# Loading the first eight rows of k as fp32 on SyncE's queue, with casts on VectorE and ScalarE, and building the identity later

## The chip, the cores and the metric

The kernel runs on one core of one Trainium2 chip. The metric is the device time of one execution in microseconds (us), lower is better. Times are compared between executions of the same rounds on the same chip.

## The reference, cut to what matters

```python
# q, k, v: (4, 6144, 256) fp32; w1, w2, w3: (256, 768); w_out: (768, 256)
qn = q / (np.linalg.norm(q, axis=1, keepdims=True) + 1e-06)
kn = k / (np.linalg.norm(k, axis=1, keepdims=True) + 1e-06)
s = kn.transpose(0, 2, 1) @ qn / tau          # 256 x 256 for each of 4 batches
a = softmax(s)                                # over the last axis
x = (v @ a).reshape(24576, 256)
out = np.maximum(np.maximum(x @ w1, x @ w2), x @ w3) @ w_out
```

## The kernel before

Only the first batch concerns us: its k and q have to be loaded, all of them, before the first attention matrix exists. k and q lie in SBUF as fp8, and the cast is done by the DMA itself; these loads are issued by GpSimd (POOL). Each partition holds 48 rows of 256 columns.

```python
k_r = k.rearrange("b (p g) c -> b p g c", p=P)          # 48 rows g per partition

def load_k(b, g0, w):
    POOL.dma_start(out=qk[b][1][:, g0:g0 + w, :], in_=k_r[b][:, g0:g0 + w, :])

for load, widths in ((load_k, [4, 4] + [8] * 5), (load_q, [8] * 5 + [4, 2, 2])):
    g0 = 0
    for w in widths:
        load(0, g0, w)
        g0 += w
        if load is load_k and g0 == 8:
            ident = consts.tile([P, P], BF16, name="ident")
            make_identity(nc, ident)                     # two instructions on GpSimd
# ... then the weights and the first v tiles, on POOL too
```

TensorE multiplies k with itself (`kk`, for the norms) as the pieces land, then q with k (`gram`), makes the weights of the first half (`aw_half`), and works through v in chunks of 512 rows. The first v tile is transposed on TensorE, all others by a transposing DMA on SyncE's queue:

```python
aw_half(et, rinv, aw, 0, [2], lambda: v_transpose_pe(0))
v_transpose(1)                                           # SP.dma_start_transpose
# ... for each chunk gi:
    load_v(gi + 4)
    v_transpose(gi + 2)
    for fc in range(FC):
        h_block(gi, aw, fc)                              # 6 matmuls of 512 columns each
        for f in gaps[fc]:
            f()
```

## Time and profile before

| | before |
|---|---|
| time, 3 runs | 586.51 us (585.48 to 586.59) |
| span of the profiled run | 584.5 us |
| TensorE busy | 95% of the span |
| first traffic on the DMA engines | 2.60 us |
| last 8-row load of k taken up by TensorE | 20.10 us |
| transpose of the second v tile landed | 56.05 us |
| from there to the end | TensorE without a gap |

A trace is read here from its end: what must be earlier for the end to be earlier? The chain of waits answers that, and the windows (busy times and DMA rate of a stretch) tell what the stage in question is short of. The prediction shows the lines. In all lines from the profile, PE is TensorE, PEld its loading of weights, DVE VectorE, ACT ScalarE, POOL GpSimd and SP SyncE; a q behind the name (SPq) means the engine's instruction queue.

### The profile page before, as it was taken

How to read it: one execution, taken by the hardware profiler on the slowest of the kernel's cores; microseconds unless marked ns; L12 is line 12 of the kernel's file. 1: busy time of each engine (PE TensorE's matmuls, PEld its weight loads, DVE VectorE, ACT ScalarE, POOL GpSimd, SP SyncE). 2: the span in 40 equal slices, each digit the busy share in tenths (PEclk: the TensorE clock that was granted, in tenths of full speed). 3: DMA queues.
4: the chain of work that ended last, by engine and by line, in shares of the span. 5: the costliest groups of instructions: out<-in, count | busy, mean ns of one | idle time of the engine just before them, and what ended most of it. 6: DMA issues, size and time to landing. Idle time of an engine off the chain costs nothing.

```text
span 584.5 us, 9286 instructions
## 1 busy us (share of the span) xinstructions
PE 557.8 (95%) x3316; PEld 327.9 (56%) x3316; DVE 405.5 (69%) x623; ACT 305.6 (52%) x526; POOL 225.3 (39%) x232
## 2 busy tenths in 40 slices
PE   2786999999999999999999999999999999999997
PEld 2652555555575555555575555555575555555554
DVE  0035678778748787777848778777857777778775
ACT  0033357676735447767646446767745444444442
POOL 4241017877671006777770105777671000000000
PEclk9998899999999999999999999999999999999999
DMA  8999927988468635888649624899646344323211
GB/s 77 107 171 163 140 56 135 141 122 155 89 118 120 105 101 94 156 131 134 124 87 145 108 83 99 125 155 133 119 91 127 73 90 117 82 58 106 55 72 73
DMA packets 75134, 64.83 MB, mean 111 GB/s; under 512 B 52304, under 2 KB 61392, under 8 KB 75088
## 3 DMA queue, kind: packets, MB, share of 16 engines
q0 software_dynamic: 18400, 26.75, 38.8%
q1 hardware_dynamic: 56544, 37.23, 24.9%
q8 instruction: 26, 0.43, 0.3%
q10 hardware_dynamic: 144, 0.26, 0.1%
q14 instruction: 20, 0.16, 0.1%
HBM read 78.64 MB, written 25.17 MB: 178 GB/s over the span
## 4 chain that ended last, share of the span: by engine, by line
PE 90%; DMA 9%; POOL 1%; issue 0%; DVE 0%; POOLq 0%
PE h_ps L320 63%; PE o_ps L339 21%; DMA q_sb<-in_q_dram 3%; PE gram L226 3%; DMA vt_sb<-v_sb 2%; PE ew_ps L273 2%; DMA k_sb<-in_k_dram 2%; DMA v_sb<-in_v_dram 1%; PE o_ps L359 0%; POOL w_sb L128 0%; POOL k_sb L99 0%; PE n_ps L207 0%; PE n_ps L209 0%; DVE o_sb L365 0%; POOL ident masks.py:199 0%
## 5 line engine op out<-in xcount | busy, mean ns | idle before, releaser
L320 PE MATMUL h_ps<-vt_sb,aw_sb 128*128 128x512 bf16 x1728 | 409.0, 381 | 5.0 <-DMA vt_sb<-v_sb 5.0
L324 DVE TENSOR_TENSOR s_mx<-h_ps,s_mx 128x512 bf16<-128x512 f32 x288 | 197.8, 687 | 105.8 <-ACT s_mx L323 98.7
L320 PEld LDWEIGHTS <-aw_sb 128*128 128x128 bf16 x1728 | 168.8, 98 | 169.9 <-DMA vt_sb<-v_sb 5.5
L323 ACT ACTIVATE s_mx<-h_ps 128x512 bf16<-128x512 f32 x288 | 171.4, 595 | 138.8 <-PE h_ps L320 137.5
L325 DVE TENSOR_TENSOR ht_sb<-h_ps,s_mx 128x512 bf16<-128x512 f32 x288 | 199.3, 692 | 30.7 <-DVE s_mx L324 0.5
L195 POOL TENSOR_TENSOR acc<-acc,sq 128x768 f32<-128x768 f32 x90 | 147.5, 1650 | 70.8 <-ACT sq L189 70.6
L339 PE MATMUL o_ps<-wo_sb,ht_sb 128*128 128x256 bf16 x1128 | 154.0, 273 | 0.0
L339 PEld LDWEIGHTS <-ht_sb 128*128 128x128 bf16 x1128 | 110.5, 98 | 53.3 <-issue 0.6
L342 ACT ACTIVATE o_sb<-o_ps 128x512 f32<-128x512 f32 x94 | 56.1, 597 | 83.0 <-PE o_ps L339 83.0
L110 POOL DMA_DIRECT2D v_sb<-in_v_dram x48 | 26.7, 559 | 105.3 <-DMA vt_sb<-v_sb 101.6
L189 ACT ACTIVATE sq<-q_sb 128x768 bf16<-128x768 fp8e4 x48 | 40.5, 844 | 0.0
L189 ACT ACTIVATE sq<-k_sb 128x768 bf16<-128x768 fp8e4 x48 | 40.1, 835 | 0.0
L192 POOL CAST acc<-sq 128x768 f32<-128x768 bf16 x6 | 4.9, 820 | 74.7 <-ACT sq L189 74.7
L102 POOL DMA_DIRECT2D q_sb<-in_q_dram x32 | 17.6, 553 | 12.4 <-DMA k_sb<-in_k_dram 11.0
L157 PE MATMUL kk<-k_sb 128*128 128x256 fp8e4 x48 | 7.8, 339 | 13.6 <-DMA k_sb<-in_k_dram 13.6
L99 POOL DMA_DIRECT2D k_sb<-in_k_dram x31 | 17.0, 551 | 1.0 <-POOLq L439 0.8
L273 PE MATMUL ew_ps<-w_sb,et 128*128 128x384 bf16 x96 | 17.1, 326 | 0.0
L276 ACT ACTIVATE aw_sb<-ew_ps,rinv 128x384 bf16<-128x384 f32 x24 | 13.8, 581 | 6.1 <-PE ew_ps L273 5.1
L226 PE MATMUL gram<-k_sb,q_sb 128*128 128x512 fp8e4 x144 | 16.8, 276 | 0.0
L226 PEld LDWEIGHTS <-q_sb 128*128 128x256 fp8e4 x144 | 15.9, 136 | 0.6
L178 ACT ACTIVATE lnk<-kb_ps 128x256 f32<-128x256 f32 x1 | 0.4, 384 | 27.6 <-PE kb_ps L175 27.6
L157 PEld LDWEIGHTS <-k_sb 128*128 128x256 fp8e4 x48 | 6.5, 182 | 14.7 <-DMA k_sb<-in_k_dram 14.7
(49 smaller groups left out, 107.7 us busy)
## 6 DMA issues: line engine op xcount, KB each, us to landing
out_dram<-o_sb SPq DMA_DIRECT2D x47, 512.0 KB, 2.9
v_sb<-in_v_dram POOLq DMA_DIRECT2D x48, 256.0 KB, 4.0
k_sb<-in_k_dram POOLq DMA_DIRECT2D x24, 192.0 KB, 5.5
q_sb<-in_q_dram POOLq DMA_DIRECT2D x24, 192.0 KB, 7.0
k_sb<-in_k_dram POOLq DMA_DIRECT2D x5, 256.0 KB, 11.1
q_sb<-in_q_dram POOLq DMA_DIRECT2D x5, 256.0 KB, 19.4
w_sb<-in_moe_w_dram POOLq DMA_DIRECT2D x6, 192.0 KB, 8.9
vt_sb<-v_sb SPq DMA_TRANSPOSE x47, 3.7
```

What stands on the lines that cost most here:

```text
L102: POOL.dma_start(out=qk[b][0][:, g0:g0 + w, :], in_=q_r[b][:, g0:g0 + w, :])
L110: POOL.dma_start(out=t, in_=v_r[gi // NCH, gi % NCH])
L189: ACT.activation(out=sq, in_=src, func=AF.Square)
L195: POOL.tensor_tensor(out=acc, in0=acc, in1=sq, op=ALU.add)
L226: PE.matmul(g[:, j * C:(j + 1) * C], lhsT=qt[:, tsl, j * P:(j + 1) * P], rhs=kt[:, tsl, :], start=(tp == 0 and j == 0), stop=(tp == NG // ...
L273: PE.matmul(ew[:, :FH], lhsT=et[:, j, ic * P:(ic + 1) * P], rhs=w_sb[m][:, j, fsl], start=(j == 0), stop=(j == CC - 1))
L320: PE.matmul(t.rearrange("p (t n) -> p t n", t=TPC), lhsT=aw[m][:, ic, fsl], rhs=vt[:, :, ic, :], start=(ic == 0), stop=(ic == CC - 1))
L323: ACT.activation(out=s_mx, in_=hp[0], func=AF.Copy)
L324: DVE.tensor_tensor(out=s_mx, in0=hp[1], in1=s_mx, op=ALU.max)
L325: DVE.tensor_tensor(out=ht[:, fc, :], in0=hp[2], in1=s_mx, op=ALU.max)
L339: PE.matmul(st["ps"][:, half], lhsT=ht[:, fc, t * P:(t + 1) * P], rhs=wo_sb[:, fc, :], start=(fc == 0), stop=(fc == FC - 1))
L342: ACT.activation(out=st["o"][:, t - 1:t + 1, :].rearrange("p t d -> p (t d)"), in_=st["ps"], func=AF.Copy)
```

## The change

The intent: SyncE has nothing to do in the first 40 us. Its queue is to bring the first eight rows of k of each partition (a sixth of k), as they are in memory (fp32), while POOL's queue starts up. VectorE and ScalarE, idle at that time, cast half of them each. The identity matrix, which GpSimd builds, leaves the start of POOL's stream.

```diff
     alloc_qk(0)
-    for load, widths in ((load_k, [4, 4] + [8] * 5), (load_q, [8] * 5 + [4, 2, 2])):
-        g0 = 0
+
+    HEAD = 8
+    kf = consts.tile([P, HEAD, C], FP32, name="kf")
+    HH = HEAD // 2
+    for i in range(2):
+        SP.dma_start(out=kf[:, i * HH:(i + 1) * HH, :], in_=k_r[0][:, i * HH:(i + 1) * HH, :])
+    for load, widths in ((load_k, [8] * 5), (load_q, [8] * 5 + [4, 2, 2])):
+        g0 = HEAD if load is load_k else 0
         for w in widths:
             load(0, g0, w)
             g0 += w
-            if load is load_k and g0 == 8:
+            if load is load_q and g0 == 8:
                 ident = consts.tile([P, P], BF16, name="ident")
                 make_identity(nc, ident)
@@ ... @@
     DVE.memset(warm, 0.0)
+
+    DVE.tensor_copy(out=qk[0][1][:, 0:HH, :], in_=kf[:, 0:HH, :], saturate=False)
+    ACT.activation(out=qk[0][1][:, HH:HEAD, :], in_=kf[:, HH:HEAD, :], func=AF.Copy, saturate=False)
```

## The prediction

> **What bounds the kernel now.** I read the page first, then the chain of waits up to 70 us, the half-microsecond windows, and the timeline of the first stage. The page puts 90% of the chain that ended last on TensorE and 9% on DMA; POOL has 1%:
>
> ```profile
> PE   2786999999999999999999999999999999999997
> ...
> PE 90%; DMA 9%; POOL 1%; issue 0%; DVE 0%; POOLq 0%
> ```
>
> From the fourth slice on (a slice is 14.6 us) TensorE is 90% busy or more, so a change in the first microseconds can only move the moment at which that steady part begins. The chain, in order of time, says what sets that moment:
>
> ```profile
> 3.01 0.49 POOL k_sb L99
> 3.50 9.21 DMA k_sb<-in_k_dram
> ...
> 12.99 20.07 DMA q_sb<-in_q_dram
> ...
> 35.54 8.08 DMA v_sb<-in_v_dram
> ...
> 43.63 12.41 DMA vt_sb<-v_sb
> ...
> 56.09 5.30 PE h_ps L320 x12
> ```
>
> To be seen (the pieces before 3.01 are the first POOL issues at 1.23 and 1.89 and the building of the identity): apart from issues, everything up to 56 us is transfers. They are k, q, the weights, v, then the transpose of the second v tile, which shares the DMA engines with loads already in the queue. TensorE waits 5.0 us for that transpose and then runs to the end. So the quantity that matters is when the DMA stream gets through a fixed amount of data.
>
> Windows (columns: stretch, its length, busy time and count of PE, PEld, DVE, ACT and POOL, PE clock, DMA share, GB/s):
>
> ```profile
> 2.00:2.50 0.50, 0.00 (x0) 0.00 (x0) 0.00 (x0) 0.01 (x1) 0.50 (x2) 1.00 0.00 0
> 2.50:3.00 0.50, 0.00 (x0) 0.00 (x0) 0.00 (x0) 0.00 (x0) 0.42 (x3) 1.00 0.78 20
> ...
> 6.00:6.50 0.50, 0.01 (x1) 0.01 (x1) 0.00 (x0) 0.00 (x0) 0.50 (x2) 1.00 1.07 61
> ...
> 2.50:10.00 7.50, 1.50 (x8) 1.13 (x8) 0.00 (x0) 0.00 (x0) 4.64 (x10) 1.00 1.01 84
> 10.00:20.00 10.00, 5.02 (x32) 4.28 (x32) 0.00 (x0) 0.00 (x0) 2.12 (x4) 1.00 1.06 107
> ```
>
> No byte moves before 2.5 us, although the first load is issued at 1.23. The GB/s count the fp8 bytes written, a quarter of the fp32 bytes read, so 107 means 428 GB/s read. That rate then holds from 10 to 30 us without a gap: the stream is limited by what is read, and the queue never runs dry. The mean from 2.5 to 10 us is only 84.
>
> **What the Trainium skill says.** "DMA: Bandwidth & Descriptors", section "Issuing engines are not separate DMA queues": DMAs issued from different engines run on the same 16 DMA engines and interleave; only the sequencer's issue time is saved. So a second queue buys no rate where the windows show 428 GB/s read, only the time in which the first queue has not begun. The trace of the kernel before agrees as far as it goes: the v transposes on SyncE are slow, 12.41 us, exactly while POOL loads are in flight.
>
> The same page, "Specifications", gives a first byte after about 1 us for the GpSimd path and 0.6 us for the SyncE path. This trace has both longer: POOL's load, issued at 1.23, shows traffic from the window at 2.5 us on; an output store, issued by SyncE at 79.05, shows its first traffic in the window 79.75 to 80.00 (229 GB/s), and 410 in the next quarter. So about 0.8 against 1.3 us; I use these.
>
> "SBUF — State Buffer", section "SBUF: two separate sides", warns that an fp32 copy on VectorE between SBUF tiles locks GpSimd out of a shared port and stalls its descriptor writing. The change adds one such copy. The kernel before has none at this place, so its trace says nothing here.
>
> "TensorE: Matmul & The Clock Gate", section "Part 1: The HAM clock gate": an idle window of about 3.4 us halves the clock, and a sustained busy one of that length restores it. This trace agrees:
>
> ```profile
> 51.20:54.60 3.40, 0.00 (x0) 0.00 (x0) 1.48 (x3) 0.00 (x0) 0.00 (x0) 1.00 1.13 115
> 54.60:58.00 3.40, 1.91 (x5) 0.74 (x6) 0.00 (x0) 0.60 (x1) 1.43 (x3) 0.51 1.17 171
> 58.00:61.50 3.50, 3.50 (x10) 1.31 (x9) 2.13 (x4) 0.60 (x1) 1.75 (x4) 0.50 1.05 120
> 61.50:65.00 3.50, 3.50 (x23) 2.10 (x22) 2.02 (x3) 1.46 (x3) 0.00 (x0) 1.00 1.10 139
> ```
>
> TensorE is idle from 51.1 to 56.1, the clock is 0.5 from about 54.65 to 61.5, and the work from 56.1 to 61.5 runs at half speed: 5.4 us, of which 2.7 are lost.
>
> **The change, part by part.**
> *Removed*: two POOL loads of k, four rows per partition each. In the chain they are issued at 1.23 and 1.89, about 0.53 us apiece, 1.2 us of POOL's stream together.
> *Moved*: the identity (0.22 and 0.29 us with gaps, 0.54 together) goes behind the first q load. VectorE needs it first at 21.5 us, so it stays hidden. POOL now issues k rows 8 to 15 at 1.23 instead of 3.0. Beyond that the order of POOL's issues is the same, and each load still waits for the landing of the one eight before it, as before.
> *Added on SyncE*: two fp32 loads of 512 KB. The other engines get past the start barrier at 0.73 to 0.83 us; SyncE should issue at about 0.8, so its first bytes come at about 0.8 + 0.8 = 1.6. The bytes read from HBM are the same as before; the writes are four times larger for this sixth of k, at 410 GB/s by the store's window, near the 428 of the stream.
> *Added casts*: VectorE's tensor ops grow from 284 ns at 128 columns to 687 at 512, about 1.05 ns a column, so 1,024 columns cost at most 1.2 us, less if the copy runs in a faster mode. ScalarE grows from 595 ns at 512 to 840 at 768, so about 1.1 us. VectorE is otherwise idle until 21.5 us and ScalarE until 29.6. The casts let TensorE begin on k, but TensorE then waits for every later 8-row load (1.2 us of every 2.46) and for the q landing, so the casts are off the path unless they last several microseconds.
>
> Gain of the stream, against full rate (107 GB/s in written bytes):
> 1. Earlier start: 2.5 to about 1.65, less 0.1 for the SyncE queue's own ramp: 0.75 us.
> 2. Ramp of the POOL queue, 2.5 to 5.5 us: six windows of 20, 49, 86, 102, 105, 104 are 233 KB against 321, so 88 KB or 0.82 us. The SyncE queue has about 0.65 of its 1 MB left then and can fill it; I take 0.7.
> 3. The dip from 5.5 to 9.5 us (86, 61, 70, 90, 94, 90, 98, 111; 350 KB against 428): 0.73 us. I see no cause for it, so I count a third, 0.25.
> Sum: 1.7 us, with a floor near 0.9 and a ceiling near 2.3. Every later transfer and TensorE's restart at 56.1 should move by that.
>
> **The clock step.** The restart meets the clock gate's windows. If their edges stay at 51.24, 54.65, 58.07 and 61.48 us (multiples of 3.41 from the span's start fit all the clock changes), then with a shift over 1.4 us TensorE restarts before 54.65, at 54.4. The window up to 54.65 is still nearly all idle, so the clock drops; the next is fully busy, so it is restored at 58.07 instead of 61.48. That loses 1.7 instead of 2.7 us and adds 1.0 to the gain: 2.7 in all. With a shift under 1.4 us the clock is restored at 61.48 as before, and half of the shift is lost at half clock: 0.5 to 0.7 gained.
>
> **Rivals.**
> (a) *Rigid shift, same clock loss*: 1.7 us gained, 584.8. For it: the loss is tied to the idle length if the windows float from run to run, as the skill page says. Against it: the runs before lie within 1.1 us, which floating windows would hardly allow.
> (b) *No throttle*: the few tenths of work before the window's edge are enough to keep the clock, or the idle gap falls across two windows. The whole 2.7 comes back: 4.4 in all, 582.1. Against it: such a window is 90% idle.
> (c) *Hidden anyway*: the two queues only interleave and the ramp is HBM's, not the queue's; shift below 1.4, gain about 0.6, 585.9. For it: the dip at 6 us comes with the queue already full.
> (d) *A new wait*: the VectorE copy holds POOL's descriptor writing, or the casts hold TensorE. At most 1.2 us at about 4 us, while several loads are queued and TensorE has slack: 0 to +0.5, up to 587. I see no engine that becomes the bound.
>
> **Range and chances.** Weights: the main line at 583.8 about 0.4, (a) 0.15, (b) 0.2, (c) 0.2, (d) 0.05. The weighted mean is 584.2. The middle eight tenths run from (b) to just past (c): 581.9 to 586.1. Two per cent is 11.7 us, several times the largest gain I can add up and more than everything before the first byte, so the chance of "same" is nearly one: 0.985, faster 0.01, slower 0.005.
>
> **What would show it.** Right: traffic from about 1.6 us; the last 8-row k load, which TensorE takes up at 20.10 now, at 18.4 (17.8 to 19.2); the 2.46 us spacing unchanged; the v transpose landing near 54.4 instead of 56.05, still about 12 us long; the clock restored near 58 us; the rest of TensorE's work equally long. The step on the ramp is wrong if traffic starts early but the last k load shifts by under 1 us; the step on the clock is wrong if the half-clock stretch is as long as before or absent. The whole is wrong if the transpose at the end of the load phase does not move with the k loads, for then something other than the stream sets it, or if the SyncE loads run well under 400 GB/s.

## The result

The changed kernel took 585.21 us (median of 4 runs, 584.16 to 585.65), the kernel before in the same rounds 586.0 us (584.98 to 586.59). The ratio is 0.9986, with a 95% interval of 0.9965 to 1.0007. A ratio is the mean time of one kernel's runs over that of the other's runs in the same rounds, so it is not quite the ratio of the medians. Executions over 1.5% slower than the fastest of the same kernel are left out of the means. Two later timings, of five executions each, gave 0.9979 (0.9967 to 0.9992) and 0.998 (0.9966 to 0.9993). The gain is therefore real but small: 0.8 to 1.3 us by the three pairs of means, and "the same" at 2%.

The chain of waits of the changed kernel, in order of time (columns: start, length, what):

```profile
1.23 1.19 POOL k_sb L99 x2
2.42 10.76 DMA k_sb<-in_k_dram
...
13.47 18.73 DMA q_sb<-in_q_dram
...
33.87 8.08 DMA v_sb<-in_v_dram
...
41.97 12.85 DMA vt_sb<-v_sb
...
54.87 4.87 PE h_ps L329 x12
```

The v load is issued 1.67 us earlier than before (33.87 against 35.54), it takes 8.08 us as before, and TensorE restarts 1.22 us earlier (54.87 against 56.09). The transpose in between took 12.85 us instead of 12.41.

The half-microsecond windows of the changed kernel (columns as in the prediction; the last is GB/s as written):

```profile
1.50:2.00 0.50, 0.00 (x0) 0.00 (x0) 0.00 (x0) 0.50 (x1) 0.50 (x2) 1.00 0.81 98
2.00:2.50 0.50, 0.00 (x0) 0.00 (x0) 0.00 (x0) 0.02 (x1) 0.50 (x2) 1.00 0.77 156
2.50:3.00 0.50, 0.00 (x0) 0.00 (x0) 0.00 (x0) 0.00 (x0) 0.50 (x2) 1.00 0.78 221
...
3.50:4.00 0.50, 0.00 (x0) 0.00 (x0) 0.00 (x0) 0.00 (x0) 0.50 (x2) 1.00 0.99 401
...
6.00:6.50 0.50, 0.12 (x1) 0.00 (x0) 0.00 (x0) 0.50 (x1) 0.50 (x1) 1.00 0.97 98
```

Until about 5 us this is fp32, so the figure is also what is read; at 6 us it is fp8, and 98 means 392 GB/s read. Traffic starts in the window at 1.5 us. The new queue needs the same two microseconds to come up to its rate as POOL's did. And the dip is gone: 98 where the kernel before had 61.

The timeline of the changed kernel's start (columns: start, length, engine, line, instruction, count, and in brackets the idle time before it and what ended it):

```profile
0.74 0.87 SPq L119 DMA_DIRECT2D kf<-in_k_dram  x2
...
4.62 0.69 DVE L152 CAST k_sb<-kf 128x1024 fp8e4<-128x1024 f32 x1 [3.34 <-DMA kf<-in_k_dram]
4.84 0.63 POOL masks.py:199 TENSOR_SCALAR_AFFINE_SELECT ident<-ident 128x128 bf16<-128x128 bf16 x1
...
5.37 0.75 PE L166 MATMUL kk<-k_sb 128*128 128x256 fp8e4 x4 [5.37 <-DVE k_sb L152]
...
5.82 1.06 ACT L153 ACTIVATE k_sb<-kf 128x1024 fp8e4<-128x1024 f32 x1 [3.80 <-DMA kf<-in_k_dram]
...
18.10 1.25 PE L166 MATMUL kk<-k_sb 128*128 128x256 fp8e4 x8 [1.21 <-DMA k_sb<-in_k_dram]
```

The first matmul starts at 5.37 us, slightly later than before (5.24), because the cast stands before it; the last piece of k is taken up at 18.10 instead of 20.10. The same line of the kernel before:

```profile
20.10 1.26 PE L157 MATMUL kk<-k_sb 128*128 128x256 fp8e4 x8 [1.20 <-DMA k_sb<-in_k_dram]
```

Following the matmuls one by one through the two traces shows where the shift was lost and won. TensorE is ahead by 2.0 us at the end of k, by 1.96 at the end of q, by 1.66 in the first v chunk, by 1.22 at the restart, by 1.76 from 62 us on, and then by 1.76 at every matmul I compared up to the last one at 578.27 us. The span is shorter by only 1.4 us (584.5 to 583.1). So 0.54 us came back at 60 us and 0.37 us were lost behind the last matmul. The first is the clock:

```profile
51.20:54.60 3.40, 0.00 (x0) 0.00 (x0) 0.00 (x0) 0.00 (x0) 0.00 (x0) 0.67 1.21 112
54.60:58.00 3.40, 3.13 (x8) 1.16 (x9) 1.04 (x2) 0.60 (x1) 2.65 (x6) 0.50 0.86 168
58.00:61.50 3.50, 3.50 (x18) 1.70 (x16) 1.74 (x4) 1.19 (x2) 0.53 (x1) 0.83 1.09 110
```

In these windows of the changed kernel the clock (third number from the end) averages 0.67 in the first stretch. If it was 1 for a time and 0.5 for the rest, it was 1 for (0.67 - 0.5) / 0.5 x 3.4 = 1.16 us and fell near 52.36; the clock records say 52.35. It came back at 59.17 us. TensorE worked 4.30 us of that time at half speed and lost 2.15 us, where it had lost 2.7 before.

The second is the end of the program. SyncE's waits for the output stores at the end, before and after (columns: total, times, longest):

```profile
SPq L453 <- DMA out_dram<-o_sb: 1.7, 2, 1.1
```

```profile
SPq L462 <- DMA out_dram<-o_sb: 2.1, 2, 1.4
```

SyncE ends the program by checking the eight counters of its and ScalarE's DMAs, one after the other. The DMAs take the counters in turn, so the two added loads move every later store two places on. In the kernel before the last two stores sit on the last two of the eight counters, and nothing is left to check when they have landed. In the changed kernel they sit on the first two. SyncE comes to them 0.4 us earlier, so its waits are longer, and the wait for the last store ends at the same distance from the last matmul (3.56 us after its start in both). But six more checks of 0.06 us each follow. From the start of the last matmul to the last instruction it is 4.39 to 4.42 us in all seven traces of kernels without the SyncE loads, and 4.77 to 4.80 us in all six with them (fast executions). No run changed this order alone.

### The profile page after: what moved, and what is told of

Its sections match the earlier page's. It is cut to its first block, busy times and chain, and to the rows that moved or that the text cites. A ratio compares the mean times of both kernels' runs of the same rounds, so it can differ in the third digit from the quotient of the medians.

```text
span 583.1 us, 9290 instructions
## 1 busy us (share of the span) xinstructions
PE 557.3 (96%) x3316; PEld 327.7 (56%) x3316; DVE 406.2 (70%) x624; ACT 306.7 (53%) x527; POOL 224.6 (39%) x230
## 4 chain that ended last, share of the span: by engine, by line
PE 90%; DMA 9%; POOL 0%; issue 0%; DVE 0%; POOLq 0%
PE h_ps L329 63%; PE o_ps L348 21%; DMA q_sb<-in_q_dram 3%; PE gram L235 3%; DMA vt_sb<-v_sb 2%; PE ew_ps L282 2%; DMA k_sb<-in_k_dram 2%; DMA v_sb<-in_v_dram 1%; PE o_ps L368 0%; POOL w_sb L134 0%; PE n_ps L216 0%; POOL k_sb L99 0%; PE n_ps L218 0%; DVE o_sb L374 0%; PE rs_ps L270 0%
## 5 line engine op out<-in xcount | busy, mean ns | idle before, releaser
L235 PE MATMUL gram<-k_sb,q_sb 128*128 128x512 fp8e4 x144 | 16.8, 276 | 0.0
L178 PE MATMUL gram<-k_sb,q_sb 128*128 128x512 fp8e4 x48 | 10.8, 322 | 3.3 <-DMA q_sb<-in_q_dram 3.3
L288 DVE TENSOR_SCALAR aw_sb<-ew_ps,rinv 128x384 bf16<-128x384 f32 x24 | 13.4, 609 | 0.5 <-PE ew_ps L282 0.5
```

The lines of the kernel that those rows point to most:

```text
L235: PE.matmul(g[:, j * C:(j + 1) * C], lhsT=qt[:, tsl, j * P:(j + 1) * P], rhs=kt[:, tsl, :], start=(tp == 0 and j == 0), stop=(tp == NG // ...
```

## The experiments

Every trace gives two measures that vary less than the times: when TensorE takes up the last 8-row load of k, and when POOL's queue has written a given amount. In the three traces of the changed kernel they lie within 0.06 and 0.08 us, but in the two traces with the identity alone moved within 0.96 and 0.26. For the second measure I count POOL's packets by their start, with 256 KB added where SyncE brought the first eight rows (6,000 KB are of 1,024 bytes here). Times of single executions carry about half a microsecond of chance. All twelve runs gave correct results. Six of them were executed once, for the trace; their times are not used.

### The kernel before, once more (before_again)

No edit.

> The kernel before, unchanged, for the repeatability of what I read from one profile. Expected: TensorE takes up the last 8-row k load at 20.10 us within 0.1, the dip in the written rate between 5.5 and 9.5 us is there again (about 88 GB/s mean against 107), the v transpose lands within 0.3 us of 56.05. If the clock gate's windows float from run to run, the half-clock stretch starts somewhere else than at 54.65 us, or with another length of work in it; if they are fixed to the start of the program, it is 54.65 again.

The last k load is taken up at 20.14 us, the rate from 5.5 to 9.5 us is 86 GB/s (88 in the first trace), and 6,000 KB are reached at 48.81 us (48.62). These repeat. The restart doesn't, quite: 56.75 us against 56.09. The half-clock stretch lies at 53.64 to 60.46 us instead of 54.65 to 61.48, and costs 1.9 us instead of 2.7. The clock's windows float.

### The identity alone moved (ident_only, ident_only_timed)

```diff
-            if load is load_k and g0 == 8:
+            if load is load_q and g0 == 8:
```

> The kernel before with one part of the change: the identity is built behind the first q load, all k loads stay on POOL. Theory 1 (the dip at 5.5 to 9.5 us comes from the identity's 0.54 us between the second and third POOL issue, which makes the third load's descriptors late): the dip shrinks or goes, the last k load is taken up at 19.4 to 19.6 us. Theory 2 (POOL's descriptors are always made too slowly for the first loads, and in the changed kernel the SyncE load gave them a head start): the dip stays, 19.9 to 20.1 us. Theory 3 (the dip belongs to the change of load size from 4 to 8 rows): the dip stays, 20.1 us.

The windows from 5.5 to 9.5 us, of the kernel before and of this one:

```profile
5.50:9.50 4.00, 1.24 (x8) 0.87 (x7) 0.00 (x0) 0.00 (x0) 1.72 (x4) 1.00 1.03 88
```

```profile
5.50:9.50 4.00, 1.82 (x12) 1.45 (x12) 0.00 (x0) 0.00 (x0) 1.92 (x6) 1.00 1.09 107
```

The dip is gone, and in the timeline of this kernel the last k load comes 1.3 us earlier than before, more than even theory 1 had allowed for:

```profile
18.81 1.25 PE L157 MATMUL kk<-k_sb 128*128 128x256 fp8e4 x8 [1.20 <-DMA k_sb<-in_k_dram]
```

The mean rate accounts for (107 - 88) / 107 x 4 us = 0.7 us of the 1.3. The rest is in the unevenness of the 16 DMA engines. TensorE takes up a load only when the slowest engine is done. In the kernel before, the engines' completion records for the third load run from 8.76 to 9.88 us, and that distance of 1.1 us stays through all the k loads; here it is 8.24 to 8.61. TensorE takes the load up at 10.27 and at 8.97 us, 0.4 us after the last record in both.

The same kernel was timed later, in five rounds.

> The identity alone moved, now timed in rounds beside the changed kernel. In the traces so far the identity's move shifts the POOL stream by 0.7 to 0.9 us (6,000 KB are reached at 47.94 us against 48.62 and 48.81), and the SyncE loads by another 0.85 us (47.09 and 47.04). Theory (the two parts are worth about the same, and both pass to the end): ratio 0.9982 to 0.9992 for this kernel, 0.9973 to 0.9985 for the changed one, 0.5 to 1 us between them. Rival (the identity is the whole gain): both kernels agree within 0.3 us. The clock's phase puts some 0.5 us of noise on each single execution.

It took 585.45 us (584.13 to 586.51) against 586.16 (585.27 to 587.37) before; the ratio is 0.9989 (0.9974 to 1.0003). By the means that is 0.7 us, but the interval does not exclude that there is no gain. The new trace has part of the dip again:

```profile
5.50:9.50 4.00, 1.27 (x8) 0.89 (x7) 0.00 (x0) 0.00 (x0) 1.66 (x5) 1.00 1.05 98
```

The last k load is taken up at 19.77 us, and the completions of the third load spread over 1.48 us. So the same kernel has two quite different traces. That fits POOL being only just ahead of the DMA engines at the third load without the SyncE loads, so that an execution can fall on either side.

### k in six loads of 8 rows on POOL (pool8)

```diff
-    for load, widths in ((load_k, [4, 4] + [8] * 5), ...
+    for load, widths in ((load_k, [8] * 6), ...
-            if load is load_k and g0 == 8:
+            if load is load_q and g0 == 8:
```

> POOL alone as before, with the identity late, and k in six loads of 8 rows instead of 4, 4 and five of 8. Theory 1 (identity): no dip, last k load at about 19.5 us, as with the identity alone moved. Theory 2 (slow descriptors): a dip is there, perhaps earlier, last k load at 19.9 to 20.3 us. Theory 3 (change of size): no dip, last k load near 19.4 us, clearly earlier than with the identity alone moved.

There is no dip (107 GB/s), and the last k load is taken up at 18.63 us, 0.18 before ident_only. The change of load size is not what makes the dip, since ident_only keeps it and has none. One execution took 583.65 us; its half-clock stretch happened to cost only 1.3 us, so I read nothing from the time.

### The SyncE loads with the identity first on POOL (sp_ident_first)

```diff
-            if load is load_q and g0 == 8:
-                ident = consts.tile([P, P], BF16, name="ident")
-                make_identity(nc, ident)
+    ident = ...; make_identity(nc, ident)      # before the loop over the loads
```

> The changed kernel with the identity built at the very front of POOL's stream, so that POOL's first load is issued some 0.6 us later. Theory: the SyncE loads keep the DMA engines busy until about 5.4 us, so POOL has time to spare: no dip, last k load taken up at 18.1 us within 0.15, and the later place of the identity is worth nothing. Rival (POOL needs all of its head start): a dip appears and the last k load comes at 18.4 to 18.8 us.

My theory missed here. The last k load is taken up at 19.06 us, about a microsecond after the changed kernel's 18.10, and the engines' completions of POOL's first load spread over 1.64 us (0.62 in the changed kernel). The rate from 5.5 to 9.5 us is 101 GB/s, and 6,000 KB are reached at 47.30 us, 0.2 after the changed kernel. Yet POOL's first load was issued only 0.19 us later (1.42 against 1.23), because the identity used time in which POOL waits anyway. Half a microsecond of lateness is thus not the explanation in this case, and I have none. It is a single trace, and a spread of this size came by chance in the second trace of ident_only (1.48 us), so chance isn't excluded; against it, five traces with the identity late behind SyncE loads (three of the changed kernel, fill_after, pet_after) all lie between 18.04 and 18.13 us.

### The identity one load later; memsets in its old place (ident_g16, memset_mid)

```diff
 ident_g16:
-            if load is load_k and g0 == 8:
+            if load is load_k and g0 == 16:
 memset_mid (on top of ident_only):
+            if load is load_k and g0 == 8:
+                idle = consts.tile([P, 2, P], BF16, name="idle")
+                for i in range(2):
+                    POOL.memset(idle[:, i, :], 0.0)
```

> The kernel before with the identity one POOL load later, between the third and the fourth k load. Theory 1 (POOL's descriptors for the third load are late when 0.5 us of other work stands before them; every further load takes the DMA engines 2.46 us and POOL 0.53 us to issue, so POOL is far ahead from then on): no dip, last k load taken up at 18.7 to 18.9 us as with the identity late. Theory 2 (any work of GpSimd's in this stretch, wherever it stands, slows the engines): a dip later, between 8 and 11 us, last k load at 19.5 us or later.

> The kernel with the identity late, and in its old place two GpSimd memsets of 128 x 128 bf16, some 0.2 us each. Theory 1 (time: any half microsecond between the second and the third load costs the dip): dip as before, last k load at 19.5 to 20.1 us. Theory 2 (the cost belongs to the identity's own instructions, the affine select with the change of GpSimd's configuration before it, not to the time): no dip, last k load at 18.7 to 19.1 us.

With the identity between the third and fourth load the rate is 104 GB/s and the last k load is taken up at 18.92 us: hardly any dip. With two plain memsets between the second and third load, the windows show the dip again, in full:

```profile
5.50:9.50 4.00, 1.36 (x8) 0.98 (x8) 0.00 (x0) 0.00 (x0) 1.94 (x5) 1.00 1.04 88
```

The last k load is taken up at 20.02 us. So it isn't the identity's own instructions that are needed. Other GpSimd work between the second and third load costs the dip, even 0.36 us of it, and one load later it costs next to nothing. These are one trace each. But over all traces the 6,000 KB separate the two kinds: with such work at the third load 48.53 (memset_mid), 48.62 and 48.81 us (before), without it 47.83 (pool8), 48.02 (ident_g16), 47.94 and 48.20 us (ident_only). The difference between the two places fits a lead that POOL doesn't have at the third load and has at the fourth: it issues a load in 0.53 us, and the engines take 2.46 us for one. What POOL is late with (the descriptors that it writes, presumably) no record here shows, and sp_ident_first doesn't fit easily.

### The changed kernel, timed again (after_again, after_timed)

No edit.

> The changed kernel, unchanged, timed in more rounds. The first trace's TensorE stream ran 1.76 us earlier than before from 62 us on, made of 1.2 us at the restart and 0.5 us of clock phase by chance. Theory (rigid shift of the restart, clock phase and the last store are noise of some tenths): ratio 0.9975 to 0.9985, that is 0.9 to 1.5 us gained. Rival (nothing gained in the mean): ratio 0.9995 to 1.0005. The clock's half-rate stretch falls at another time than 52.35 to 59.17 us if its windows float.

585.09 us (583.86 to 585.35) against 586.1 (585.23 to 586.62), ratio 0.9979: 1.1 us, the theory of a rigid shift. The half-clock stretch lies at 53.21 to 60.04 us this time and costs 2.85 us.

> The changed kernel beside it, same chip, same rounds. Theory: 0.5 to 1 us faster than with the identity alone moved, ratio 0.9973 to 0.9985. Rival: the same as that kernel within 0.3 us.

584.85 us (584.56 to 585.3) against 586.16, ratio 0.998. Beside it, ident_only_timed was slower by 0.6 us in the means (585.45 against 584.85). That agrees with two parts of about equal worth, though the intervals overlap. The traces are sharper. 6,000 KB of the POOL stream are reached at:

| kernel | us | mean |
|---|---|---|
| before | 48.62, 48.81 | 48.72 |
| identity alone moved | 47.94, 48.20 | 48.07 |
| changed | 47.09, 47.04, 47.01 | 47.05 |

Added in this order, the identity's move is worth about 0.65 us and the SyncE loads 1.0, together 1.67. The other order was not run: the SyncE loads with the identity left at its old place in POOL's stream. They may well remove the dip by themselves, and then the same 1.67 us would be split otherwise. (With the identity at POOL's front, sp_ident_first gave up 0.25 us.) Less the 0.37 us at the end, 1.3 us are left, and the three timings found 0.8 to 1.3.

### Matmuls of no use in the wait (fill_after)

```diff
+            if gi == 0:
+                def fill():
+                    f_ps = htile("fill_ps")
+                    for i in range(20):
+                        PE.matmul(f_ps, lhsT=ident, rhs=warm, start=(i == 0), stop=(i == 19))
+                gaps[5].append(fill)
```

> The changed kernel with 20 matmuls of no use put into the 5.4 us in which TensorE waits for the transpose of the second v tile (about 4.3 us of work). Theory (the clock gate halves the clock in that wait and the work after it loses 2.2 to 2.7 us): no half-clock stretch after 30 us, 2 to 2.7 us faster than the changed kernel, ratio against before 0.993 to 0.995. Rival (the restart's half clock costs nothing because something else limits it then): same as the changed kernel, 0.9985.

582.48 us (582.28 to 582.64), ratio 0.9937. That is 2.5 us less than the changed kernel in the same rounds (means 584.93 and 582.47). The clock records show no half-clock stretch between 26 and 578 us, and the windows after the wait run at full clock:

```profile
54.60:58.00 3.40, 3.40 (x20) 1.86 (x19) 2.12 (x4) 1.19 (x2) 3.12 (x6) 1.00 0.93 157
```

TensorE restarts at 54.40 us, within the changed kernel's 54.25 to 54.87. So the half clock after the wait costs what the arithmetic says. The spread is also small, 0.36 us over five executions where the changed kernel had 1.5, which fits the clock's floating windows as a main source of the scatter.

### The second v tile transposed on TensorE (pet_after, pet_before)

```diff
-    v_transpose(1)
...
+            if gi == 0:
+                gaps[4].append(lambda: v_transpose_pe(1))
```

> The changed kernel with the second v tile transposed on TensorE (behind the fifth block of the first chunk) instead of by the DMA queue of SyncE. Theory (the steady part starts when that transpose lands, and it lands late because it shares the DMA engines with loads in the queue): TensorE's wait of 5.4 us and the half-clock stretch go, for about 0.6 us of transposes: 5.4 + 2.2 - 0.6 = 7 us faster than the changed kernel, near 578.5, ratio 0.986 to 0.989, unless the third v tile's transpose becomes the next wait. Rival (the next transfer is as late): a gain of 0 to 3 us only, TensorE waits for the third tile.

578.62 us (578.08 to 579.08), ratio 0.9874: 7.5 us less than before and 6.3 less than the changed kernel, by the means. The windows of this kernel show no wait and no half clock:

```profile
51.20:54.60 3.40, 3.40 (x21) 1.85 (x19) 2.83 (x6) 1.20 (x3) 0.21 (x1) 1.00 1.00 154
54.60:58.00 3.40, 3.40 (x24) 2.09 (x23) 2.45 (x4) 1.34 (x3) 2.97 (x6) 1.00 0.70 99
```

The third tile's transpose, by DMA as before, is in time. This version beats both kernels. The place at which the steady part starts was worth several times the start of the loads. Why that transpose was late can be read from the later ones in the trace before: with no POOL load in flight they land 3.6 to 3.7 us after their issue, with some 0.26 to 0.29 MB of POOL's loads beside them after about 6 us, and the second tile's, beside 1.6 MB, after 12.41.

> The kernel before with the same edit, so that the change can be read without the transpose and the clock stretch. Theory (the stream's shift of 1.55 us, 1.66 at the v loads, then passes to the end undiminished): this kernel is 1.5 to 1.8 us slower than the changed kernel with the edit, so its ratio is 0.989 to 0.992. Rival (the change is worth nothing past the first stage): the two kernels with the edit agree within 0.5 us.

579.42 us (median), ratio 0.9884 from three executions, 579.13 to 579.44. That is 0.7 us more than pet_after by the means (579.32 and 578.60), so my theory expected too much (1.5 to 1.8) and the rival too little (under 0.5). The theory had left out the 0.37 us at the end, with which 1.3 would be due. Two of pet_after's four executions have a granted clock of 0.995 and 0.996, the other two and pet_before's three have 0.999 or 1.000; between those the difference is 1.07 us (578.25 and 579.32). What the rest is I can't say: the profiled execution of pet_before was a fourth one, which ran nearly all its length at about half clock (992.94 us, granted clock 0.567). No other execution did that, and I have no cause for it.

## Why the prediction was right, and where it wasn't

The measured 585.21 us lies in the stated range, 1.0 us above the predicted 584.2, and "same" was right. But the forecast gain was 2.3 us (586.5 to 584.2), and the three timings found 0.8 to 1.3. The sum for the stream was nearly right, 1.7 us forecast against 1.53 in the first pair of traces and 1.67 in the means. That is partly luck: two of its terms were wrong in opposite directions.

**The path was right.** The restart at 56 us follows the DMA stream: 56.09 and 56.75 us in the two traces before, 54.87, 54.34 and 54.25 in the three of the changed kernel, 1.9 us between the means. After it, TensorE's work changes only by the clock. The constant shift of 1.76 us over 500 us of matmuls shows it, and pet_after shows that the transpose is the last link.

**Earlier start, 0.75 us: right.** The first packet comes at 1.77 us instead of 2.60, 0.83 earlier.

**Ramp, 0.7 us: wrong.** I had SyncE's queue fill the ramp of POOL's. Its own ramp is as long (98, 156, 221 GB/s in its first three windows, where I had taken a store's quick start in mid-kernel as the pattern). And the queues didn't share the engines: POOL's first packet comes only at 4.77 us, when SyncE's loads are nearly through (their last packet ends at 5.48). Rival (c) had said this of the ramp, that it isn't the queue's own. Counting what was read by 10 us, from the packet records (a byte of fp8 counts as four read), it is 2,764 KB with the identity alone moved and 3,124 in the changed kernel. At 428 GB/s the 360 KB between them are 0.84 us, for which the earlier first packet (0.83) accounts alone. (The second trace of the former kernel, with 2,650 KB, would make it more; no run isolates the ramp.) The prediction's signs were mixed here: the last k load moved by 2.0 us, by which the ramp step would have passed, but ident_only's first trace has 1.3 us of that from the dip. And the SyncE loads, taken whole, ran at 283 GB/s (1,049 KB from 1.77 to 5.48 us), well under the 400 named as a sign that the whole is wrong; they reached 400 only from 3.5 us on.

**Dip, a third of 0.73 us: undersized, and by a wrong step.** I wrote that the identity "stays hidden" because VectorE needs it only at 21.5 us. That is true of the identity's result, not of its place in POOL's stream. Moving it took away the whole dip in one trace (2,466 to 2,764 KB by 10 us, 0.70 us) and part of it in the other (2,650 KB), and memset_mid shows that other GpSimd work there brings it back. The change's smaller part, which I had thought worth nothing, is alone worth 0.65 us of the 1.67.

**The clock step, 1.0 us: wrong.** I took the windows to be fixed to the start of the program because one trace fitted multiples of 3.41 us. In the eleven traces that have the wait, the clock fell anywhere between 51.67 and 56.19 us, while TensorE's restart moved only between 54.25 and 56.75. The half-clock stretch was two windows long (6.83 us) in eight of them, all three of the changed kernel's among these, and one window (3.41 us) in three; so the shorter stretch that I had forecast for this change comes by chance, and those three traces (ident_only, pool8, memset_mid) are all without the SyncE loads. The skill page does call the windows free-running. By trace the loss was 2.7 and 1.9 us before, 2.15, 2.85 and 2.1 in the changed kernel. The rigid shift of rival (a) is what took place, with the clock as noise.

**Casts off the path: right.** VectorE's took 0.69 us (0.69 to 0.81 in the six traces that have it), under the 1.2 I had as a limit. The Trainium skill's "VectorE: DVE Perf Modes", section "Side-by-side: where the cycles go for N=2048 bf16", counts about 158 cycles and, in the mode of two elements a cycle, half a cycle per element, at 0.96 GHz; by that an estimate for 1,024 elements is 670 / 0.96 = 698 ns, and the trace has 694. That the cast ran in this mode is only what the match suggests. The lock that the SBUF page describes fits what is seen: the affine select that overlapped this cast took 0.62 to 0.64 us in all five traces where it did, and 0.29 in all others. It cost the stream nothing visible.

**The end of the program** was not in the prediction. It takes back 0.37 us.

## What to carry to other kernels

Ask of a load phase where its first gap is and who issues the loads: here half a microsecond of work in the issuing engine's stream delayed the stream by 0.65 us, though its result wasn't needed for a long time. Then ask what the load phase ends in, since here the last transfer of that phase (and the half clock behind it) was worth 6.3 to 6.8 us where the earlier start was worth one. Two added transfers went with a loss of 0.37 us hundreds of microseconds later, which the order in which the program's end checks them would explain. And a sum that comes out right does not show that its terms are right: only the runs that took one part each told the ramp from the dip.

## What the Trainium skill lacked or had wrong

- "DMA: Bandwidth & Descriptors", section "Queues, rings and completion order", has each DMA engine take turns between its queues, packet by packet. Equal turns agree with the transposes beside the loads at 50 us (64 packet records of POOL's and 67 of SyncE's in one microsecond of the trace before). It doesn't tell why POOL's first packet, at 2.60 us when alone, came at 4.64 to 4.82 us in the six traces with the SyncE loads in front.
- The same page, "Specifications", has first bytes after 1 and 0.6 us. Here it was 1.37 us from POOL's issue (1.23 to 2.60) and 1.03 from SyncE's (0.74 to 1.77) at the start of the program.
- No page that I read tells of the slow first two microseconds: whichever of the two queues starts, the rate read reaches about 400 GB/s only some 1.5 us after its first packet (402 GB/s between 1.5 and 2 us in the changed kernel, 408 in the kernel before).
- No page that I read says that 0.36 us of GpSimd work between the second and third load costs the stream 0.4 to 0.6 us by 10 us (2,491 against 2,650 and 2,764 KB read in the two traces without it) and the slowest DMA engine 0.25 to 1.2 us (20.02 against 19.77 and 18.81 us for the last k load).
- No page that I read has the end of a program check eight DMA counters in a fixed order at 0.06 us each: 0.37 us between ends that differ in the two added loads.
- "TensorE: Matmul & The Clock Gate", section "Part 1: The HAM clock gate", is confirmed: windows of 3.41 us that float (the clock fell at 51.67 to 56.19 us). One execution at about half clock almost throughout (992.94 us; its clock record reads 0.56 of full from 27 us on) is beyond what it describes there.
